# Linear attention and spectral mixing on one core: spectral weights loaded two modes at a time in 16 KB runs, with the two modes on row halves of TensorE

## The chip, the cores and the metric

The kernel runs on one core of a Trainium2 chip. The metric is the device time of one execution in microseconds (us). Each run also has a profiled span, which is about 1.8 us shorter than its time; the traces below are read in that span, and times "at" some microsecond count from its start. The granted clock is the share of full speed that the throttle gives TensorE.

Before the change the kernel took 427.29 us (median of 3 runs, 427.12 to 427.82).

## The reference

A linear attention (feature map elu + 1) makes x of 8 batches x 576 rows x 512 channels. A real Fourier transform along the rows follows; its first 64 modes are multiplied by complex 512 x 512 weights, one matrix pair per mode; the inverse transform is added to x, and a channel product with a rectifier ends it.

```python
x = attention(q, k, v)                     # 8 x 576 x 512
X = np.fft.rfft(x, axis=1)
Xr, Xi = X[:, :64].real, X[:, :64].imag
Yr = einsum('bmd,mde->bme', Xr, w_r) - einsum('bmd,mde->bme', Xi, w_i)
Yi = einsum('bmd,mde->bme', Xr, w_i) + einsum('bmd,mde->bme', Xi, w_r)
Y[:, :64] = Yr + 1j * Yi                   # the other modes are zero
u = x + np.fft.irfft(Y, n=576, axis=1)
return u + np.maximum(u @ w_ch, 0.0)
```

The weights are 64 modes x 2 matrices x 1 MB of float32, 134 MB of the 164 MB that the core reads.

## The kernel before

Three stages overlap. The *first stage* (to about 103 us) makes x batch by batch and transforms it. The *weights stage* multiplies mode after mode, as the weights arrive. The *tail* handles the last modes and the output after the last weights have landed.

A weight load is 1 MB, cast from float32 to bf16 on its way, on the gpsimd queue. Each partition receives four matrix rows, an 8 KB run in memory. Twelve buffers are filled in the first stage, eight more ("keep") stay in use to the end.

```python
    W_KEEP = 8
    def w_load(kk, half, pool, tag, bufs):
        name, src = (("wr", moe_w_r), ("wi", moe_w_i))[half]
        w = pool.tile([128, NDC, D], BF16, tag=tag, bufs=bufs, name=f"{name}{kk}")
        rows_of = src[kk].rearrange("(p dc) e -> p dc e", dc=NDC)          # NDC = 4
        for dcs in (slice(0, 3), slice(3, 4)) if (kk, half) == (NM - 1, 1) else (slice(0, NDC),):
            tc.keep_in_program_order(nc.gpsimd.dma_start(out=w[:, dcs], in_=rows_of[:, dcs, :]))
        return w
    W_PRE = 12
```

The transform of a batch puts channel 4p + dc on partition p of channel group dc. A group is five matmuls: four over 128 rows of x, and one over the 64 rows that are left of 576. The stationary operand (the one that TensorE loads before it streams the other) is x itself, every fourth channel.

```python
    def transform(b, dc):
        # ... cut: xf = a PSUM tile [128, 4, 2, 64]; half = the 64 partitions that hold the left rows
        o = xf[:, dc].rearrange("p t m -> p (t m)")
        for jj in range(NJJ):                                              # NJJ = 4
            pin(nc.tensor.matmul(o, x16[:, jj, dc::NDC], fwd_sb[:, jj, :], start=(jj == 0), stop=False))
        pin(nc.tensor.matmul(o, x16t[half, dc::NDC], fwd_sb[half, NJJ, :], start=False, stop=True))
        if dc == NDC - 1:
            # ... cut: two copies to xt_c, as bf16 (real, imaginary, minus imaginary)
```

The products of a mode are 8 matmuls of 128 rows x 32 columns, four of which stand side by side in the array. A product's four blocks are then added up by a 16-column "row-pick" matrix.

```python
    def mode_product(kk, ps, stage, yt_ps):
        wr, wi = w_get(kk)
        P = ps.tile([128, D], F32, tag="P", bufs=2, name=f"P{kk}")
        for t, w in ((1, wr), (0, wi)):
            for dc in range(NDC):
                fixed(nc.tensor.matmul(P[dc * 32 : dc * 32 + 32, :], xt_cols(dc, t, kk), w[:, dc, :],
                                       start=(t == 1), stop=(t == 0), tile_position=(0, dc * 32)))
            # ... cut: other work and warming matmuls
        # ... cut: P copied to st, on VectorE for even modes and ScalarE for odd ones
        for ec in range(NDC):
            fixed(nc.tensor.matmul(yt_ps[:, ec, kk % 8, :], st[:, ec * 128 : ec * 128 + 128], pick_sb))
```

The row-pick matrix is loaded on the gpsimd queue after all the prefetched weights:

```python
    while pending:
        w_next()
    tc.keep_in_program_order(nc.gpsimd.dma_start(out=wch16, in_=moe_w_ch.rearrange("(c p) j -> p c j", p=128)))
    tc.keep_in_program_order(nc.gpsimd.dma_start(out=pick_sb, in_=pick_dr.ap()))
```

Of the kernel before, what the change touches and what calls it, by code (L numbers as in the profile page):

```python
# [20 lines left out]
def _dft_consts(S: int, NM: int):  # L21

    m = np.arange(NM)
    s_cols = np.concatenate([4 * np.arange(128) + jj for jj in range(4)] + [512 + np.arange(NP)])
    s_rows = np.concatenate([s_cols, s_cols[512:]]).reshape(5, 128).T
    ang = 2.0 * np.pi * s_rows[:, :, None] * m / S
    fwd = np.concatenate([np.cos(ang), -np.sin(ang)], axis=2)

    scale = np.where(m == 0, 1.0, 2.0) / S
    ang = 2.0 * np.pi * np.outer(m, np.arange(S)) / S  # L30
    inv = np.empty((NM, 2, S), dtype=np.float64)
    inv[:, 0, :] = np.cos(ang) * scale[:, None]
    inv[:, 1, :] = -np.sin(ang) * scale[:, None]
    pick = np.zeros((128, 16), dtype=np.float16)
    for quad in range(4):
        for c in range(16):
            pick[quad * 32 + c, c] = 1.0

    return fwd.astype(np.float16), inv.reshape(2 * NM, S).astype(np.float16), pick
# [3 lines left out]
def kernel(  # L43
# [18 lines left out]
    XDC = 3 * B * NM  # L62
    XTW = NDC * XDC + 2 * B * NM
# [15 lines left out]
    fwd_sb = const.tile([128, 5, 2 * NM], F16, name="fwd_sb")  # L79
# [7 lines left out]
    nc.vector.memset(xt_c[:, NDC * XDC : XTW], 0.0)  # L87
    xt_v = xt_c[:, 0 : NDC * XDC].rearrange("p (c t b m) -> p c t b m", c=NDC, t=3, b=B)

    def xt_cols(dc: int, t: int, kk: int):  # L90

        c0 = dc * XDC + t * B * NM + kk
        return xt_c[:, c0 : c0 + 31 * NM + 1 : NM]
# [7 lines left out]
    W_KEEP = 8  # L101

    def w_load(kk: int, half: int, pool, tag: str, bufs: int):
        name, src = (("wr", moe_w_r), ("wi", moe_w_i))[half]
        w = pool.tile([128, NDC, D], BF16, tag=tag, bufs=bufs, name=f"{name}{kk}")
        rows_of = src[kk].rearrange("(p dc) e -> p dc e", dc=NDC)
        for dcs in (slice(0, 3), slice(3, 4)) if (kk, half) == (NM - 1, 1) else (slice(0, NDC),):
            tc.keep_in_program_order(nc.gpsimd.dma_start(out=w[:, dcs], in_=rows_of[:, dcs, :]))  # L108
        return w
# [4 lines left out]
    W_PRE = 12  # L114
# [170 lines left out]
    def transform(b, dc):  # L285
        if dc == 0:
            xfs[b] = psA.tile([128, NDC, 2, NM], F32, tag="xf", bufs=2, name=f"xf{b}")
        xf = xfs[b]
        o = xf[:, dc].rearrange("p t m -> p (t m)")
        half = HALVES[b % 2]  # L290
        x16, x16t = x16s[b]
        for jj in range(NJJ):
            pin(
                nc.tensor.matmul(
                    o, x16[:, jj, dc::NDC], fwd_sb[:, jj, :], start=(jj == 0), stop=False
                )
            )
        pin(
            nc.tensor.matmul(
                o, x16t[half, dc::NDC], fwd_sb[half, NJJ, :], start=False, stop=True  # L300
            )
        )
        if dc == NDC - 1:
            pin(nc.vector.tensor_copy(out=xt_v[:, :, 1:3, b, :], in_=xf))
            pin(nc.scalar.mul(out=xt_v[:, :, 0, b, :], in_=xf[:, :, 1, :], mul=-1.0))
# [7 lines left out]
    for b in range(B):  # L313
        if b + 2 < B:
            load(b + 2)
            if b >= 1:
                w_next()
# [29 lines left out]
    FILL = {61: (2, 2, 1), 62: (5, 3, 3), 63: (6,)}  # L347

    def mode_product(kk: int, ps, stage, yt_ps):

        wr, wi = w_get(kk)
        st = stage.tile([128, D], F16, tag="ystage", bufs=2, name=f"ys{kk}")
        fixed = pin if kk >= NF else (lambda ins: ins)
        fill = FILL.get(kk, (0, 0, 0))
        P = ps.tile([128, D], F32, tag="P", bufs=2, name=f"P{kk}")
        for t, w in ((1, wr), (0, wi)):
            for dc in range(NDC):
                fixed(
                    nc.tensor.matmul(  # L359
                        P[dc * 32 : dc * 32 + 32, :], xt_cols(dc, t, kk), w[:, dc, :],  # L360
                        start=(t == 1), stop=(t == 0), tile_position=(0, dc * 32),
                    )
                )
            if t == 1:
                work_slot(kk, 0)
                keep_warm(fill[0])
        if kk % 2 == 0:
            fixed(nc.vector.tensor_copy(out=st, in_=P))  # L368
        else:
            fixed(nc.scalar.copy(out=st, in_=P))  # L370
        work_slot(kk, 1)
        keep_warm(fill[1])
        for ec in range(NDC):
            fixed(
                nc.tensor.matmul(  # L375
                    yt_ps[:, ec, kk % 8, :], st[:, ec * 128 : ec * 128 + 128], pick_sb
                )
            )
# [10 lines left out]
    def last_mode(ps):  # L389

        kk = NM - 1
        wr, wi = w_get(kk)
        y_last = ps.tile([128, NDC, 2 * B], F32, tag="P", bufs=2, name="y_last")

        def product(t, w, dcs):
            for dc in dcs:
                c0 = dc * XDC + t * B * NM + kk
                x = xt_c[:, c0 : c0 + (2 * B - 1) * NM + 1 : NM]
                for ec in range(NDC):
                    pin(  # L400
                        nc.tensor.matmul(
                            y_last[:, ec, :], w[:, dc, ec * 128 : ec * 128 + 128], x,
                            start=(t == 1 and dc == 0 and ec == 0), stop=(t == 0 and dc == NDC - 1),
                            skip_group_check=True,
                        )
                    )

        product(1, wr, range(NDC))
        keep_warm(FILL[kk][0])
        product(0, wi, range(3))  # L410
        product(0, wi, range(3, NDC))
        nc.vector.tensor_copy(out=Y8[:, :, NL - 1, :], in_=y_last)
# [14 lines left out]
    n_early = n_keep + n_pre  # L427
# [28 lines left out]
    def mode(kk: int):  # L456
        nonlocal yt_ps
        if kk % 8 == 0:
            yt_ps = psW.tile([128, NDC, 8, 2 * B], F32, tag="yt", bufs=1, name=f"yt{kk // 8}")
        if kk == NM - 1:  # L460
            last_mode(psW)
            return
        mode_product(kk, psW, ystage, yt_ps)
        if kk == NM - 2:
            pin(nc.vector.tensor_copy(out=Y8[:, :, 0 : NL - 1, :], in_=yt_ps[:, :, 0 : NL - 1, :]))
        elif kk % 8 == 7:
            if kk < NF:
                nc.vector.tensor_copy(out=YE_T[:, :, kk - 7 : kk + 1, :], in_=yt_ps)
            else:
                g = (kk - NF) // NL + 1  # L470
                pin(nc.vector.tensor_copy(out=YL[:, :, :, g, :], in_=mode_rows(yt_ps)))

    for kk in range(n_early):
        mode(kk)
# [232 lines left out]
    QUADS = (5, 6)  # L707
# [52 lines left out]
    for kk in range(n_early, NM):  # L760
        mode(kk)
        if kk < NF:
            for i in spread(len(tiles), kk - n_early, NF - n_early):
                attention_rows(tiles[i])
        if kk == NE + 4:
            assert not work
            psB.release()
            acc_pools.append(
                tc.alloc_tile_pool(name="psT0", bufs=1, space=PSUM, side="right", reuse_waits="tile")
            )  # L770
            per_slot[NE + 5] = [1, 1]
            for n in range(N_PRE):
                work.append(lambda n=n: channels(n))

# [100 lines left out]
```

## Time and profile before

| | before |
|---|---|
| profiled span | 425.4 us |
| queue of the loads, share of 16 engines | 98.3% |
| written by the DMA engines, 160 to 340 us | 213 GB/s |
| transform of one batch (20 matmuls), clock 0.5 | 3.1 us |
| first product of the weights stage | 103.4 us |
| last product of the last mode | 393.1 us |
| from there to the end | 32.3 us |

The page of the kernel before. Part 2 cuts the span into 40 slices and gives the busy share in tenths per engine and the bytes written; part 3 lists the DMA queues with packets, MB and share of 16 engines; part 4 is the chain of waits that ended last, by engine.

```profile
PE   1358777887119765666333689778677778998992
...
DVE  4598999956002755556200433433444244421793
...
GB/s 215 208 208 209 209 210 209 212 212 215 218 211 214 214 212 215 214 213 214 212 214 213 213 214 213 214 214 213 213 213 214 214 213 213 213 213 157 250 394 295
...
q0 software_dynamic: 31360, 81.48, 98.3%
...
DMA 69%; PE 12%; issue 8%; DVE 7%; ACT 2%; POOL 1%; DVEq 0%; POOLq 0%; ACTq 0%
```

The gpsimd queue is busy for 98% of the span, at a level rate from the start to about 390 us (the last packet of the weights ends at 392.7 us), and 69% of the chain of waits is DMA. So the loads bound the kernel, and TensorE and VectorE may be late as long as the queue does not run empty. In the first stage VectorE is the busier one, as the windows of the kernel before show (columns: window, its length, busy us and instructions of PE, weight loads, VectorE, ScalarE and GpSimd, then granted clock, DMA share and GB/s written):

```profile
60.00:100.00 40.00, 30.56 (x434) 23.58 (x429) 32.62 (x64) 21.60 (x29) 9.73 (x17) 0.66 1.13 211
...
160.00:340.00 180.00, 118.71 (x935) 59.42 (x934) 71.56 (x173) 46.37 (x81) 38.12 (x72) 0.72 1.06 213
```

```profile
395.00:400.00 5.00, 4.75 (x22) 2.05 (x20) 3.96 (x6) 3.92 (x8) 0.56 (x1) 1.00 0.68 206
```

### The profile page before, as it was taken

To read this page: it belongs to the slowest core of one execution; us is meant where nothing else is said; L and a number is where in the kernel's file an instruction comes from. 1 tells how busy PE (TensorE), PEld (TensorE's weight loads), DVE (VectorE), ACT (ScalarE), POOL (GpSimd) and SP (SyncE) were. 2 spreads that over 40 slices of the span, in tenths; PEclk is the share of its full clock that TensorE was granted. 3 is DMA by queue.
4 is the path that set the end of the run, shared out by engine and by line. 5 is a ranking of instruction groups with operands and counts; after the bars stand their busy time and mean duration, and the time that the engine had idled before them with its cause. 6 is when DMAs were issued, how large, how long until landed. Compare 5 with 4: busy or idle time off the path is not lost.

```text
span 425.4 us, 6619 instructions
## 1 busy us (share of the span) xinstructions
PE 285.7 (67%) x2692; PEld 160.0 (38%) x2692; DVE 214.5 (50%) x440; ACT 154.1 (36%) x241; POOL 88.3 (21%) x159
## 2 busy tenths in 40 slices
PE   1358777887119765666333689778677778998992
PEld 0246555674003433333111334434334334473420
DVE  4598999956002755556200433433444244421793
ACT  4677776630102100000000244434443354430781
POOL 4222223222201322122112122112122121110000
PEclk9999866565555855555555587989999899999998
DMA  9999999999999999999999999999999999998797
GB/s 215 208 208 209 209 210 209 212 212 215 218 211 214 214 212 215 214 213 214 212 214 213 213 214 213 214 214 213 213 213 214 214 213 213 213 213 157 250 394 295
DMA packets 35502, 93.12 MB, mean 219 GB/s; under 512 B 3024, under 2 KB 15696, under 8 KB 35216
## 3 DMA queue, kind: packets, MB, share of 16 engines
q0 software_dynamic: 31360, 81.48, 98.3%
q1 hardware_dynamic: 4112, 11.22, 7.1%
q8 instruction: 21, 0.34, 0.3%
q14 instruction: 9, 0.07, 0.0%
HBM read 163.93 MB, written 9.44 MB: 407 GB/s over the span
## 4 chain that ended last, share of the span: by engine, by line
DMA 69%; PE 12%; issue 8%; DVE 7%; ACT 2%; POOL 1%; DVEq 0%; POOLq 0%; ACTq 0%
DMA wi<-in_moe_w_i_dram 51%; DMA wr<-in_moe_w_r_dram 9%; DMA k<-in_k_dram 9%; PE acc L641 3%; PE P L359 2%; DVE x L277 2%; PE acc L680 2%; ACT ke L190 1%; PE z L604 1%; DVE ke L203 1%; DVE k L197 1%; PE zb L631 1%; PE zb L630 1%; DVE qe L203 1%; PE yb L626 1%
## 5 line engine op out<-in xcount | busy, mean ns | idle before, releaser
L359 PE MATMUL P<-wi,xt_c 128*32 128x512 bf16 x252 | 37.9, 536 | 38.7 <-DMA wi<-in_moe_w_i_dram 38.6
L370 ACT CAST ys<-P 128x512 f16<-128x512 f32 x31 | 18.2, 586 | 121.6 <-PE P L359 106.8
L108 POOL DMA_DIRECT2D wr<-in_moe_w_r_dram x64 | 34.1, 533 | 130.6 <-PE P L359 91.0
L368 DVE CAST ys<-P 128x512 f16<-128x512 f32 x32 | 22.1, 691 | 72.0 <-PE P L359 49.8
L108 POOL DMA_DIRECT2D wi<-in_moe_w_i_dram x65 | 34.6, 532 | 111.8 <-PE P L359 88.2
L359 PEld LDWEIGHTS <-xt_c 128*32 128x32 bf16 x504 | 28.7, 156 | 75.8 <-issue 64.4
L359 PE MATMUL P<-wr,xt_c 128*32 128x512 bf16 x252 | 37.6, 550 | 24.6 <-DMA wr<-in_moe_w_r_dram 22.5
L563 DVE TENSOR_TENSOR x_main<-ya,x_main 128x512 f32<-128x512 f32 x32 | 22.1, 691 | 43.7 <-PE ya L559 43.6
L582 PE MATMUL eps<-wch,xTw 128*128 128x512 f16 x144 | 41.2, 414 | 0.0
L144 PEld LDWEIGHTS <-qT 64*128 64x128 f16 (+1 forms) x640 | 25.3, 126 | 41.6 <-issue 21.3
L565 ACT CAST x16w<-x_main 128x512 f16<-128x512 f32 x32 | 19.8, 618 | 37.4 <-DVE x_main L563 37.4
L375 PE MATMUL yt<-pick_sb,ys 128*128 128x16 f16 x252 | 16.6, 176 | 24.1 <-DMA pick_sb<-row_pick 15.2
L590 ACT CAST E<-eps 128x512 f16<-128x512 f32 (+1 forms) x40 | 21.3, 543 | 25.5 <-PE eps L582 25.5
L144 PE MATMUL num<-kv,qT 64*128 64x65 f16 (+1 forms) x320 | 13.8, 227 | 20.7 <-ACT kv L250 18.0
L375 PEld LDWEIGHTS <-ys 128*128 128x128 f16 x252 | 12.3, 103 | 39.8 <-issue 16.6
L190 ACT ACTIVATE qe<-q 128x1152 f16<-128x1152 f16 (+1 forms) x16 | 17.8, 1157 | 17.8 <-DMA q<-in_q_dram 17.8
L219 PE MATMUL qTp<-id,qe 128*128 128x128 f16 x144 | 16.7, 309 | 10.1 <-DVE qe L203 9.5
L144 PE MATMUL nw<-kv,qT 64*128 64x65 f16 (+1 forms) x320 | 22.1, 236 | 1.6 <-DVE x_tail L533 1.0
L277 DVE TENSOR_TENSOR x<-num,rd 128x512 f16<-128x512 f32 x32 | 22.1, 692 | 1.1
L190 ACT ACTIVATE ke<-k 128x1152 f16<-128x1152 f16 x16 | 17.7, 1155 | 6.6 <-DMA k<-in_k_dram 6.0
L690 ACT ACTIVATE acc<-acc 128x512 f32<-128x512 f32 x34 | 18.1, 581 | 2.3 <-PE acc L641 1.3
L219 PEld LDWEIGHTS <-qe 128*128 128x128 f16 x144 | 14.5, 146 | 11.2 <-DVE qe L203 9.9
(104 smaller groups left out, 442.5 us busy)
## 6 DMA issues: line engine op xcount, KB each, us to landing
wr<-in_moe_w_r_dram POOLq DMA_DIRECT2D x64, 512.0 KB, 18.6
wi<-in_moe_w_i_dram POOLq DMA_DIRECT2D x63, 512.0 KB, 18.7
k<-in_k_dram POOLq DMA_DIRECT2D x8, 576.0 KB, 14.5
v<-in_v_dram POOLq DMA_DIRECT2D x8, 576.0 KB, 16.6
out_dram<-x_main SPq DMA_DIRECT2D x9, 512.0 KB, 3.1
q<-in_q_dram POOLq DMA_DIRECT2D x7, 576.0 KB, 13.8
out_dram<-x_main SPq DMA_DIRECT2D x2, 1024.0 KB, 5.2
out_dram<-x_main SPq DMA_DIRECT2D x6, 256.0 KB, 3.4
```

Source lines behind the costliest of these rows:

```text
L108: tc.keep_in_program_order(nc.gpsimd.dma_start(out=w[:, dcs], in_=rows_of[:, dcs, :]))
L144: mm = nc.tensor.matmul(num[hpo][orow, c0 : c0 + 65], qT[rows, hpp, h2, cols], kv_sb[rows, hpp, h2, :])
L190: pin(nc.scalar.activation(out=ev[:, c], in_=heads(nm, b, c), func=AF.Exp))
L219: nc.tensor.transpose(qT_ps[:, j].rearrange("p t r -> p (t r)"), phi["q", b][:, hpp, j].rearrange("p o d -> p (o d)"), id16,)
L277: nc.vector.tensor_tensor(out=dst.rearrange("p (o c d) -> p o c d", o=2, c=4), in0=nv[:, :, :, 0:64], in1=rden.unsqueeze(3).broadcast_to([ ...
L359: nc.tensor.matmul(P[dc * 32 : dc * 32 + 32, :], xt_cols(dc, t, kk), w[:, dc, :], start=(t == 1), stop=(t == 0), tile_position=(0, dc * 32),)
L368: fixed(nc.vector.tensor_copy(out=st, in_=P))
L375: nc.tensor.matmul(yt_ps[:, ec, kk % 8, :], st[:, ec * 128 : ec * 128 + 128], pick_sb)
L563: pin(nc.vector.tensor_tensor(out=x, in0=acc, in1=x, op=ALU.add))
L565: pin(nc.scalar.copy(out=x16w[t], in_=x))
L582: nc.tensor.matmul(e_ps, xT[:, c, :], wch16[:, c, :], start=(c == 0), stop=(c == NDC - 1))
L590: pin(nc.scalar.copy(out=dst, in_=e_ps[:, cols]))
```

## The change

The intent: fewer and longer packets. Two modes are loaded at once, so that a partition receives eight matrix rows of one mode, a 16 KB run; even modes lie on partitions 0 to 63, odd ones on 64 to 127. 128 loads of 1 MB become 64 of 2 MB. The price is on TensorE. The channels of a mode now lie on 64 partitions (channel 8p + dc, eight groups), so the transform needs 80 matmuls of 64 columns per batch instead of 20 of 128, each with every eighth channel as stationary operand; and a pair of modes needs 32 product matmuls of 64 rows instead of 16 of 128. The last load comes in four pieces instead of two.

```diff
-    fwd = np.concatenate([np.cos(ang), -np.sin(ang)], axis=2)
+    fwd = np.stack([np.cos(ang), -np.sin(ang)], axis=2)
+    fwd = np.stack([fwd[..., 0::2], fwd[..., 1::2]], axis=2)
 ... cut
-    W_KEEP = 8
+    W_KEEP = 4
+    PIECES = (slice(0, 4), slice(4, 6), slice(6, 7), slice(7, 8))
-    def w_load(kk: int, half: int, pool, tag: str, bufs: int):
+    def w_load(kp: int, half: int, pool, tag: str, bufs: int):
-        w = pool.tile([128, NDC, D], BF16, tag=tag, bufs=bufs, name=f"{name}{kk}")
-        rows_of = src[kk].rearrange("(p dc) e -> p dc e", dc=NDC)
+        w = pool.tile([128, NDW, D], BF16, tag=tag, bufs=bufs, name=f"{name}{kp}")
+        rows_of = src[2 * kp : 2 * kp + 2].rearrange("k (p dc) e -> (k p) dc e", dc=NDW)
 ... cut
-    W_PRE = 12
+    W_PRE = 6
 ... cut: transform
-        for jj in range(NJJ):
-            pin(nc.tensor.matmul(o, x16[:, jj, dc::NDC], fwd_sb[:, jj, :], start=(jj == 0), stop=False))
-        pin(nc.tensor.matmul(o, x16t[half, dc::NDC], fwd_sb[half, NJJ, :], start=False, stop=True))
+        for dc in (2 * step, 2 * step + 1):
+            o = [xf[HALVES[h], dc].rearrange("p t m -> p (t m)") for h in range(2)]
+            for jj in range(NJJ + 1):
+                rows = half if jj == NJJ else slice(0, 128)
+                x = x16t[half, dc::NDW] if jj == NJJ else x16[:, jj, dc::NDW]
+                for h in range(2):
+                    pin(nc.tensor.matmul(o[h], x, fwd_sb[rows, jj, h].rearrange("p t m -> p (t m)"),
+                                         start=(jj == 0), stop=(jj == NJJ), skip_group_check=True))
 ... cut: the products of a pair
-            for dc in range(NDC):
-                nc.tensor.matmul(P[dc * 32 : dc * 32 + 32, :], xt_cols(dc, t, kk), w[:, dc, :], ...)
+            for dc in range(NDW):
+                c = dc % NDC * 32
+                for h in range(2):
+                    nc.tensor.matmul(P[h][c : c + 32, :], xt_cols(dc, t, kp)[HALVES[h]], w[HALVES[h], dc, :],
+                                     ..., tile_position=(h * 64, c), skip_group_check=True)
 ... cut
-    FILL = {61: (2, 2, 1), 62: (5, 3, 3), 63: (6,)}
+    FILL = {NM // 2 - 2: (2, 2, 3), NM // 2 - 1: (4,)}
```

FILL counts the matmuls without use ("warming matmuls") that are meant to keep TensorE's clock up near the end; e10 and e11 below compare two counts. The cut parts carry the pairs through the rest of the kernel.

## The prediction

> **What bounds it now.** The loads on the gpsimd queue. The page gives that queue 98% of 16 engines' span, and the chain of waits is 69% DMA. From 20 to 390 us the trace's packet records never show fewer than 16 packets in flight: no engine idles. In the weights stage (windows 160 to 380 us) 213 GB/s are written, 426 GB/s read, since the load halves float32 to bf16. The last weights land at 393 us; the 32 us after it (output) are untouched.
>
> **Cost of one load.** In the packet records a 2,304-byte read takes 107 ns, an 8,192-byte read 324 ns, a completion packet 22 ns. That is 22 ns + 0.0369 ns/byte: 434 GB/s for 16 engines, which agrees with the 435 GB/s fabric ceiling in the Trainium skill ("DMA: Bandwidth & Descriptors", "Where 436 GB/s comes from"). A 1 MB load (8 packets and a completion per engine) takes about 2,461 ns, less than 8 x 324 + 22 = 2,614, so each packet hides about 19 of its 22 ns. Left over the pure byte time are 8 x 3 + 22 = 46 ns per load. The same sum gives 2,835 ns for the q, k, v loads; their 208 GB/s agree. So the queue is within 2% of its ceiling; the prize is small.
>
> **On the critical path.** 128 loads become 64 of twice the size: a saved completion and, if a 16 KB run stays one packet, eight saved packets per pair. Estimate 64 x 46 ns = 2.9 us. If runs are cut back to 8 KB (the same page, "SDMA does more than copy", names 2,048 elements as the limit of one unit, CCE; no trace here shows whether it holds for a casting load), only completions are saved: 1.4 us.
>
> **Off the critical path.**
> - Products: 32 matmuls of 64 rows per pair in place of 16 of 128. Four old ones run together in 0.40 us at full clock (timeline). Eight tiles should run together: neutral.
> - Transforms: 80 half-size matmuls a batch in place of 20. Old: 3.1 us a batch at clock 0.65; estimate 4 to 6 us. TensorE is 73% busy there, VectorE 95%, so the first stage may end 3 to 10 us later than 103 us. It has room: prefetched weights keep the queue filled to about 123 us, and q, k, v loads wait 11 us behind others.
> - Buffers: 4 of 2 MB instead of 8 of 1 MB. When one is freed three stand queued, 14.7 us; TensorE lags 1 to 5 us in the busiest part. Enough.
> - Tail after the last landing: 8 small matmuls for 4, two parallel evictions: +0.2 us. Fewer warming matmuls may cost clock there: up to 2 us, unlikely.
>
> **Prediction.** 427.3 - 2.3 (between the two cases) + 0.2: 425.2 us, range 423.0 to 428.0. Faster by over 2%: 0.02; within 2%: 0.94; slower by over 2%: 0.04.
>
> **What would show it.** Right: written rate in the weights windows rises from 213 to about 215 GB/s; weight packets of 8,192 written bytes at about 626 ns; last weights land near 390.5 us; at least 16 packets in flight throughout; 32 us of tail. Split case: 4,096-byte packets remain, rate about 214.
>
> **What would make it wrong.** Gaps in the queue before 125 us because the transforms made TensorE the limit of the first stage (slower by several us); products of 64 rows running in turn, so that TensorE, 85 to 100% busy from 350 us, frees buffers late; a clock drop before the tail; long packets sharing engines unevenly.

## More of the kernel before

The timeline of TensorE in the kernel before, at the end of the first stage (start and length in us; the lengths of matmuls overlap, so read the distance between starts):

```profile
100.56 0.62 PE L294 MATMUL xf<-fwd_sb,x 128*128 128x128 f16 x4
...
101.34 0.62 PE L294 MATMUL xf<-fwd_sb,x 128*128 128x128 f16 x4
101.89 0.29 PE L299 MATMUL xf<-fwd_sb,x16t 64*128 64x128 f16 x1
103.38 0.68 PE L359 MATMUL P<-wr,xt_c 128*32 128x512 bf16 x4 [1.20 <-ACT xt_c L305]
```

One channel group, five matmuls, takes 0.78 us from start to start (100.56 to 101.34) at clock 0.5. The first product starts 1.5 us after the last transform.

The timeline of GpSimd's issues in the kernel before. In brackets stands how long it sat idle and what released it:

```profile
111.04 0.53 POOL L108 DMA_DIRECT2D wr<-in_moe_w_r_dram  x1 [2.21 <-DMA wr<-in_moe_w_r_dram]
...
127.84 0.54 POOL L108 DMA_DIRECT2D wr<-in_moe_w_r_dram  x1 [8.90 <-PE rows L512]
...
140.40 0.53 POOL L108 DMA_DIRECT2D wr<-in_moe_w_r_dram  x1 [9.71 <-PE P L359]
```

The load at 111.04 us is the 21st, so the first that needs a used buffer (20 are prefetched). The first two modes are multiplied at 103.4 to 105.3 us, which frees four buffers, and the loads into them go out from 111.04 to 118.41 us, held only by the queue itself. The two later lines are loads that do wait for a buffer. The queue stays filled meanwhile: no slice up to 380 us falls below 208 GB/s.

The tail of the kernel before, as the instructions on the result tile of the last mode (shortest, median and longest ns, first and last start), and the clock after it in the windows:

```profile
L401 PE MATMUL y_last<-xt_c,wi x16: 188/192/193, 392.4 to 393.1; 128*128 128x16 bf16 x16
```

## The result, and the profile after

| | before | after |
|---|---|---|
| time, median of 6 runs (lowest to highest) | 427.56 us (427.12 to 428.33) | 435.02 us (433.90 to 436.72) |
| profiled span | 425.4 us | 432.2 us |
| share of the load queue | 98.3% | 94.2% |
| written, 160 to 340 us | 213 GB/s | 216 GB/s |
| transform of one batch at clock 0.5 | 3.1 us | 7.05 us |
| first product of the weights stage | 103.4 us | 127.3 us |
| last product of the last mode | 393.1 us | 399.0 us |
| from there to the end | 32.3 us | 33.2 us |

The changed kernel is slower by 1.7%, so still within 2%: ratio 1.0173, 95% interval 1.0149 to 1.0198. A ratio here and below is the mean time of the one kernel's runs over the mean of the other's runs of the same rounds, so not quite the ratio of the medians. Executions over 1.5% slower than the fastest of the same kernel are left out of the means.

The page of the changed kernel, with the same lines as above except the chain of waits, which breaks off early in this profile (its shares sum to 10% of the span) and is not used:

```profile
PE   1259999999989855555523387887597768996992
...
DVE  4595787766321536546530153444245333531794
...
GB/s 215 207 208 212 207 214 205 217 215 215 215 106 196 207 207 215 214 218 215 215 216 215 216 217 213 216 216 217 214 217 215 217 215 215 215 215 134 221 400 304
...
q0 software_dynamic: 22432, 81.47, 94.2%
```

The queue's rate is up in the weights stage (mostly 214 to 217 where mostly 213 or 214 stood), with far fewer packets, and one slice has a hole: 106 GB/s, from 119 to 130 us. In the eight slices before it PE stands at 9, and VectorE, which had mostly stood at 9 in the first of them, is at 5 to 8. The windows of the changed kernel say the same in numbers:

```profile
60.00:100.00 40.00, 38.03 (x532) 33.31 (x530) 29.94 (x56) 21.63 (x27) 9.26 (x15) 0.56 1.11 213
100.00:120.00 20.00, 19.33 (x274) 16.74 (x274) 8.81 (x20) 3.43 (x6) 0.00 (x0) 0.59 1.03 216
120.00:130.00 10.00, 8.80 (x105) 6.03 (x106) 2.72 (x14) 0.73 (x3) 0.96 (x2) 0.50 0.51 93
130.00:150.00 20.00, 17.75 (x237) 6.57 (x235) 5.56 (x12) 5.17 (x12) 2.13 (x5) 0.50 1.01 206
160.00:340.00 180.00, 112.44 (x1276) 51.80 (x1275) 76.99 (x196) 43.14 (x77) 19.56 (x37) 0.68 1.03 216
```

TensorE is busy for 38.0 of 40 us between 60 and 100 us (30.6 before), and for nearly all of the next 20 us, in which the kernel before let it rest. The timeline of TensorE in the changed kernel, at the end of its first stage:

```profile
124.23 0.69 PE L302 MATMUL xf<-fwd_sb,x 128*64 128x64 f16 x8
...
125.11 0.69 PE L302 MATMUL xf<-fwd_sb,x 128*64 128x64 f16 x8
125.74 0.33 PE L302 MATMUL xf<-fwd_sb,x16t 64*64 64x64 f16 x2
127.27 1.09 PE L365 MATMUL P<-wr,xt_c 64*32 64x512 bf16 x16 [1.20 <-ACT xt_c L309]
```

A group of ten matmuls takes 0.88 us (124.23 to 125.11), so eight groups take 7.05 us per batch where four took 3.1. The first product comes at 127.27 us, 23.9 us later. The timeline of GpSimd's issues in the changed kernel shows what that does:

```profile
93.05 0.54 POOL L428 DMA_DIRECT2D pick_sb<-row_pick  x1 [4.20 <-DMA wi<-in_moe_w_i_dram]
128.69 0.53 POOL L112 DMA_DIRECT2D wr<-in_moe_w_r_dram  x1 [35.10 <-PE P L365]
...
133.76 0.53 POOL L112 DMA_DIRECT2D wr<-in_moe_w_r_dram  x1 [3.66 <-PE P L365]
...
148.68 0.53 POOL L112 DMA_DIRECT2D wr<-in_moe_w_r_dram  x1 [13.49 <-PE P L365]
```

From 93 us on every buffer has its load landed or queued. The first load into a used buffer goes out at 128.69 us, after the first products (in the kernel before, at 111.04 us); but the queue had run dry at about 123.5 us (171 GB/s in the window of 121 to 124 us, 10 GB/s in that of 124 to 127). A second, shorter hole lies near 147 us. There the early modes are worked off one pair every 3.56 us (product starts at 139.32, 142.88 and 146.44 us).

**Where the time went.** The bytes on the load queue, added up over the trace, give the lag of the queue without a model. The yardstick is kernel e10 below, the same loads with no hole. The changed kernel's queue is level with it at 20 MB, 6.8 us behind after the first hole (at 25 MB) and 7.9 us behind after the second (at 30 MB); it stays 7.8 us behind to the end. The kernel before is 2.8 us behind e10 at the end. So:

| term | us |
|---|---|
| longer packets, fewer completions | -2.8 |
| first hole | +6.8 |
| second hole | +1.0 |
| last pieces of the last load | +0.9 |
| tail after the last product | +0.9 |
| sum | +6.8 |

The difference of the profiled spans is 432.2 - 425.4 = 6.8 us. The lags are good to about 0.2 us. The fourth term is what is left between the queue (+5.0 us) and the last product (+5.9 us). Its cause is open. In the packet records a fetch of 16 KB of instructions on another queue, about 0.95 us long, falls on those last small pieces in the changed kernel (396.77 to 397.71 us; the last packet ends at 398.51); but such a fetch falls among the last small pieces of e10 too (388.43 to 389.37, last packet 389.78), of e1, s1 and s3, where these pieces are not late against the rest of the queue, and of the kernel before (last packet at 392.65 us; 392.63 in e2, which has no fetch there). So the fetch alone does not explain it.

The tail of the changed kernel, in the two views that were shown of before:

```profile
L408 PE MATMUL y_last<-xt_c,wi x64: 184/187/196, 396.3 to 399.0; 64*128 64x16 bf16 x64
```

```profile
395.00:400.00 5.00, 2.97 (x73) 1.86 (x72) 0.23 (x1) 0.24 (x2) 0.00 (x0) 0.59 0.30 52
```

The clock fell to 0.59 in those 5 us, where it had been 1.00: TensorE waits between four pieces with few warming matmuls. The four matmuls of the last channel product that follow take 1.06 us in the timeline, 0.60 us before.

### The profile page after: what moved, and what is told of

It reads as the page before. It is cut to its first block, busy times and chain, and to the rows that moved or that the text cites. A ratio compares the mean times of both kernels' runs of the same rounds, so it can differ in the third digit from the quotient of the medians.

```text
span 432.2 us, 8601 instructions
## 1 busy us (share of the span) xinstructions
PE 312.9 (72%) x3741; PEld 183.5 (42%) x3741; DVE 213.0 (49%) x439; ACT 153.5 (36%) x242; POOL 55.6 (13%) x97
## 2 busy tenths in 40 slices
DMA packets 26725, 93.24 MB, mean 216 GB/s; under 512 B 2048, under 2 KB 14848, under 8 KB 18496
## 3 DMA queue, kind: packets, MB, share of 16 engines
q0 software_dynamic: 22432, 81.47, 94.2%
## 5 line engine op out<-in xcount | busy, mean ns | idle before, releaser
L365 PE MATMUL P<-wr,xt_c 64*32 64x512 bf16 x496 | 34.6, 554 | 38.2 <-DMA wr<-in_moe_w_r_dram 34.6
L365 PE MATMUL P<-wi,xt_c 64*32 64x512 bf16 x496 | 32.0, 535 | 32.0 <-DMA wi<-in_moe_w_i_dram 32.0
L365 PEld LDWEIGHTS <-xt_c 64*32 64x32 bf16 x992 | 18.7, 147 | 80.1 <-issue 51.4
L591 PE MATMUL eps<-wch,xTw 128*128 128x512 f16 x144 | 44.4, 440 | 0.0
L302 PE MATMUL xf<-fwd_sb,x 128*64 128x64 f16 x512 | 44.2, 309 | 0.0
L112 POOL DMA_DIRECT2D wr<-in_moe_w_r_dram x32 | 17.4, 545 | 161.1 <-PE P L365 122.2
L302 PEld LDWEIGHTS <-x 128*64 128x64 f16 x512 | 35.9, 212 | 4.1
L112 POOL DMA_DIRECT2D wi<-in_moe_w_i_dram x35 | 18.6, 534 | 103.5 <-PE ya L568 38.9
L302 PE MATMUL xf<-fwd_sb,x16t 64*64 64x64 f16 x128 | 20.7, 321 | 0.0
L591 PEld LDWEIGHTS <-xTw 128*128 128x128 f16 x144 | 14.1, 110 | 15.2 <-issue 8.2
```

The costliest lines, as they stand in the source:

```text
L302: nc.tensor.matmul(o[h], x, fwd_sb[rows, jj, h].rearrange("p t m -> p (t m)"), start=(jj == 0), stop=(jj == NJJ), skip_group_check=True,)
L365: nc.tensor.matmul(P[h][c : c + 32, :], xt_cols(dc, t, kp)[HALVES[h]], w[HALVES[h], dc, :], start=(t == 1 and dc < NDC), stop=(t == 0 and ...
L591: nc.tensor.matmul(e_ps, xT[:, c, :], wch16[:, c, :], start=(c == 0), stop=(c == NDC - 1))
```

## The experiments

The expectations are quoted; they name theories by letter. A is that the longer transforms make the first stage late and the queue run dry. B, its rival, is that half as many buffers of twice the size come free too late or too coarsely. D, W and L in the last four runs are rival reasons for the price of one transform matmul. Times are medians of all runs of a kernel, with the lowest and highest in brackets; the kernel before ran in each set of rounds, at medians of 427.36 to 427.64 us.

### e1: the changed kernel with a shorter transform

Two of the five row blocks are multiplied, so 32 matmuls per batch instead of 80. The result is wrong; the comparison is too loose to see the spectral term.

```diff
-            for jj in range(NJJ + 1):
+            for jj in (0, NJJ):
```

> The changed kernel with each transform cut to 2 of its 5 row groups (32 matmuls a batch instead of 80, about 2.8 us instead of 7.05; the result is wrong on purpose, all loads, buffers and products unchanged). Theory A (the longer transforms make TensorE the limit of the first stage, so the first buffers are freed at 128.7 us, after the prefetched weights have run out at 123.5 us): the first stage ends near 103 us, no gap in the load queue, time 424.5 to 426.5 us. Rival B (4 buffers of 2 MB are freed too coarsely, or long packets share the engines badly): the gap near 125 to 150 us stays and the time stays at 432 us or more.

Measured: 427.69 us (427.45 to 428.48), ratio 1.0005 [0.9993, 1.0018]. The issues of e1 in the timeline of GpSimd:

```profile
109.34 0.53 POOL L112 DMA_DIRECT2D wr<-in_moe_w_r_dram  x1 [15.65 <-PE P L365]
...
128.90 0.53 POOL L112 DMA_DIRECT2D wr<-in_moe_w_r_dram  x1 [18.15 <-PE P L365]
...
143.81 0.53 POOL L112 DMA_DIRECT2D wr<-in_moe_w_r_dram  x1 [13.48 <-PE P L365]
```

The first hole is gone and about 7 us with it, with the loads, buffers and products of the change left alone: A holds for the first hole. The time expected was missed by 1.2 us, since the second hole grew. The queue ends 2.3 us behind e10, the tail's clock is low, and the gain of the packets is used up by that. The first buffers come free early here, but the next not before 128.90 us: the early products wait for the row-pick matrix, which lands at about 125 us, and then run at clock 0.50 (windows of 130 to 150 us).

### e2: the kernel before with a longer transform

Each channel group is multiplied two or three times over, 45 matmuls per batch instead of 20, with the right result.

```diff
-        for jj in range(NJJ):
-            pin(...)
-        pin(...)
+        for _ in range(3 if dc == 0 else 2):
+            for jj in range(NJJ):
+                pin(...)
+            pin(...)
```

> The kernel before with its transforms computed 2.25 times (45 matmuls a batch instead of 20, about 7.0 us; right result), loads and buffers as before. Theory A: the first stage ends near 125 us, a gap of 4 to 8 us in the load queue, time 432 to 437 us although no load was changed. Rival B: the queue stays full, time within 1 us of 427.5.

Measured: 426.95 us (426.86 to 427.02), ratio 0.9985 [0.9972, 0.9998]. A miss. The timeline of TensorE and a window of e2 say why:

```profile
107.21 0.41 PE L295 MATMUL xf<-fwd_sb,x 128*128 128x128 f16 x4
...
107.74 0.41 PE L295 MATMUL xf<-fwd_sb,x 128*128 128x128 f16 x4
...
109.53 0.47 PE L360 MATMUL P<-wr,xt_c 128*32 128x512 bf16 x4 [1.20 <-ACT xt_c L306]
```

```profile
60.00:100.00 40.00, 32.40 (x550) 25.31 (x551) 33.67 (x65) 22.68 (x30) 9.66 (x17) 1.00 1.13 211
```

The extra matmuls brought the clock from 0.66 to 1.00, and five of them then took 0.53 us instead of 0.78. The stage ended about 6 us later than before, not 24, and no hole came. So the count of matmuls alone is not the cost. What differs in the changed kernel is that its ten matmuls take 0.88 us at any clock: also between 33 and 43 us, where the clock is 1.00.

### e3 and e5: the kernel before with loads of two modes

These test B: 2 MB loads and half as many buffers, with the old transform and products. e3 keeps 8 KB runs and is right; e5 has the 16 KB runs of the change and is wrong (the rows of two modes get mixed).

```diff
+        w = pool.tile([128, 2, NDC, D], BF16, tag=tag, bufs=bufs, name=f"{name}{kp}")
+        rows_of = src[2 * kp : 2 * kp + 2].rearrange("k (p dc) e -> p k dc e", dc=NDC)            # e3
+        rows_of = src[2 * kp : 2 * kp + 2].rearrange("k (p dc) e -> (k p) dc e", dc=2 * NDC)      # e5
 ... cut: W_KEEP 4, W_PRE 6, one load per pair
```

> The kernel before with two modes per load (2 MB, 4 buffers instead of 8) but runs of 8 KB and the old layout, transforms and products. Theory A: no gap; only 64 completions of 22 ns are saved, time 1.0 to 1.8 us below before, written rate about 214 GB/s. Rival B (coarse buffers cause the gap): a gap appears and the time rises by 3 us or more.

> As the 8 KB pair load, but the loads are those of the changed kernel (16 KB runs, even modes on partitions 0 to 63), with the old transforms and products on it, so the result is wrong on purpose. Theory A: no gap, written rate about 216 GB/s, time 2.4 to 3.4 us below before (424.1 to 425.1). Rival C (long packets cost something themselves, for example uneven engines): no gain over the 8 KB runs, or a loss.

Measured: e3 433.55 us (428.52 to 436.05, two of six runs slow), ratio 1.0081 [1.0038, 1.0123] from the fast ones, which fall into two groups, near 428.5 and near 433.5 us (the profiled run is of the upper one); e5 429.92 us (427.35 to 432.39), ratio 1.0061 [1.0031, 1.0090]. Two windows of e5 and one of e3:

```profile
120.00:130.00 10.00, 4.93 (x42) 1.82 (x41) 0.69 (x1) 1.97 (x5) 0.89 (x2) 0.50 1.11 217
...
160.00:340.00 180.00, 116.15 (x928) 55.76 (x929) 71.11 (x170) 45.79 (x82) 19.03 (x36) 0.70 1.03 216
```

```profile
380.00:385.00 5.00, 5.00 (x52) 3.56 (x50) 0.85 (x2) 1.76 (x3) 1.45 (x3) 0.76 0.37 45
```

Neither has a hole at 123 us, so B does not explain the first one. Nor has either the second hole, though their row-pick matrix is as late (first used at 125.1 and 125.4 us); their clock from 130 to 140 us was 0.93 (e5) and 0.67 (e3), where the changed kernel had 0.50. The 16 KB runs bring the rate to 216 GB/s (e3: 214), which confirms the gain that the change was made for. But coarse buffers do cost something in *these* kernels: near the end, with the products still one mode at a time, a pair's buffer comes free late and the queue rests (45 GB/s in e3's window of 380 to 385 us). In the changed kernel both modes of a buffer are multiplied back to back, and no such hole is there.

### e6: e1 with the row-pick matrix loaded early

```diff
                 pin(nc.sync.dma_start(out=fwd_sb, in_=fwd_dr.ap()))
+                pin(nc.sync.dma_start(out=pick_sb, in_=pick_dr.ap()))
 ...
-    tc.keep_in_program_order(nc.gpsimd.dma_start(out=pick_sb, in_=pick_dr.ap()))
```

> The short-transform kernel of the first series (wrong on purpose) with one more edit: the 4 KB row-pick matrix is loaded at the start on the sync queue instead of behind all prefetched weights, so the early pairs need not wait for it until about 125 us. Theory A2 (what was left of the loss there was a second gap of 3.3 us near 144 us, because the early pairs are worked off too late, and a slow clock at the start of the tail): no gap before 390 us, time about 424.5 us (424.0 to 425.5). Rival B (coarse buffers themselves): the gap of about 3 us stays and so does 427.7.

Measured: 426.69 us (426.44 to 427.32), ratio 0.9983 [0.9971, 0.9995]. The second hole is gone: the windows from 120 to 150 us show 213 GB/s or more, and the queue is level with e10 to the end. The expected time was missed by about 1.2 us: the last piece comes 0.9 us later than in e10 (last packet at 390.71 us, last product at 391.5 us; why is open, see above), and the clock is 0.50 in the window of 390 to 395 us. With both holes removed the time falls below the kernel before, with a transform cut short; e10 below repeats it with a whole one.

### e4: the changed kernel with more warming matmuls near the end

```diff
-    FILL = {NM // 2 - 2: (2, 2, 3), NM // 2 - 1: (4,)}
+    FILL = {NM // 2 - 2: (2, 2, 8), NM // 2 - 1: (5,)}
-        for dcs in PIECES:
+        for i, dcs in enumerate(PIECES):
             product(0, wi, dcs)
+            keep_warm((2, 1, 0, 0)[i])
```

> The changed kernel with 9 more clock-keeping matmuls between the last two pairs and between the pieces of the last load. Theory A: the clock before the last landing stays at 1.00 instead of 0.59, the stretch from the last landing to the end is 32.4 us instead of 33.4, time 0.5 to 1.3 us below the changed kernel (433.7 to 434.5), with the gaps near 125 and 150 us unchanged. Rival: the time does not move, the tail is bound by VectorE.

Measured: 433.62 us (431.12 to 435.94), ratio 1.0141 [1.0115, 1.0166], which overlaps that of the change (1.0149 to 1.0198, in other rounds): inconclusive. The clock stayed at 1.00 until 400 us but fell to 0.66 in the next 5 us, after TensorE had waited 1.35 us for the last piece. The profiled run holds something else, which no edit made, as the edit lies near the end. Its clock happened to be high after the first hole:

```profile
130.00:150.00 20.00, 13.18 (x262) 6.68 (x261) 7.21 (x15) 5.33 (x12) 3.09 (x6) 0.93 1.02 204
```

Its queue, 7.2 us behind e10 after the first hole, was only 0.2 us further behind at 30 MB, where the changed kernel at clock 0.50 lost 1.0 us. This is one execution, but it suggests that the slow clock has a large part in the second hole.

### e7 and e8: full-width transforms, with x written in another order

Here x is written so that each group's 128 channels lie side by side; 20 full-width matmuls per batch do, and copies move halves of the result across partitions. e8 adds the early row-pick load and the warming.

```diff
+        dv = dst.rearrange("p (u o c e) -> p o c e u", u=NDW, o=2, c=4)
+        for o in range(2):
+            pin(nc.vector.tensor_tensor(out=dv[:, o], in0=..., in1=..., op=ALU.mult))
 ... cut
-                x = x16t[half, dc::NDW] if jj == NJJ else x16[:, jj, dc::NDW]
+            x = x16t[half] if jj == NJJ else x16[:, jj]
+            pin(nc.tensor.matmul(o, x[:, g * 128 : g * 128 + 128], fwd_sb[rows, jj]..., ...))
```

> The changed kernel with 20 full-width transforms a batch again (right result): the channels are permuted when x is written, and four half-partition copies, two of them from one row half to the other, put even modes on rows 0 to 63 and odd ones on 64 to 127. Theory A (number of weight loads of the half-width transforms is what made the first stage long; loads and buffers are innocent of the first gap): first stage ends before 110 us, no gap near 125 us, the second gap of 2 to 4 us stays, time 426.5 to 428.5 us. Rival (moving data between row halves costs as much): the stage stays beyond 120 us and the time above 432.

> Full-width transforms, early row-pick matrix and warm tail together, 16 KB loads kept (right result). Theory A: no gap in the load queue before the last landing, 216 GB/s written, last weights near 390.3 us, tail 32.5 us, time 424.3 to 425.3 us, 0.5 to 0.8% below the kernel before. Rival B: one of the gaps comes back and the time stays at or above 427.

Measured: 485.88 us (485.69 to 486.22), ratio 1.1366 [1.1351, 1.1381], and 486.74 us (483.69 to 488.35), ratio 1.1370. Both failed. The groups of instructions of e7 on VectorE:

```profile
L283 DVE TENSOR_TENSOR x<-num,rd 128x256 f16<-128x256 f32 x64 | 78.0, 1406 | 1.6
```

Two such writes, whose neighbours lie 128 bytes apart, take 2.8 us where one contiguous write of 128 x 512 took 0.69 us. VectorE, in the kernel before already 95% busy from 30 to 60 us, became the bound, and the queue stood empty for tens of microseconds. Moving a stride from one engine to another can be dearer than the stride.

### e10 and e11: the transform swapped

The transform first runs with the Fourier matrix as stationary operand (five matmuls of 512 columns), ScalarE copies the result, and 16 half-width matmuls with the identity turn it. e10 also loads the row-pick matrix early; e11 adds the warming.

```diff
+                pin(nc.tensor.matmul(xfs[b], fwd_sb[rows, jj].rearrange("p h t m -> p (h t m)"),
+                                     x16t[half] if jj == NJJ else x16[:, jj],
+                                     start=(jj == 0), stop=(jj == NJJ)))
 ... cut: after the five, on ScalarE
+                pin(nc.scalar.copy(out=xms[b], in_=xfs[b]))
 ... cut: for dc in the 8 groups, for h in both halves
+                pin(nc.tensor.matmul(xf[HALVES[h], dc].rearrange("p t m -> p (t m)"),
+                                     xms[b][:, dc::NDW], id16[:, h * 64 : h * 64 + 64], ...))
 ... cut: e11 only
-    FILL = {NM // 2 - 2: (2, 2, 3), NM // 2 - 1: (4,)}
+    FILL = {NM // 2 - 2: (2, 2, 8), NM // 2 - 1: (5,)}
+            keep_warm((3, 1, 1, 0)[i])
```

> The changed kernel with the same layout and loads (right result), but each batch's transform made in another order: 5 wide matmuls (Fourier matrix stationary, 512 channels moving) give modes on rows, one ScalarE copy rounds them to fp16, and 16 half-width matmuls with the identity put channels back on rows, even modes low and odd modes high; 21 weight loads a batch instead of 80, about 3.5 us instead of 7.05. The row-pick matrix is loaded at the start. Theory A: first stage ends before 110 us, no gap in the load queue near 125 or 145 us, 216 GB/s written, time 425.0 to 427.0 us, below the kernel before by up to 0.6% and 7 to 10 us below the changed kernel. Rival B (the coarse buffers are to blame): a gap of 3 us or more remains and the time is 428 or more.

> The swapped transform with more clock-keeping matmuls around the last pair. Theory A: clock 1.00 in the first 5 us after the last landing and a tail 0.5 to 1.0 us shorter than that of the swapped transform alone: 424.5 to 426.3 us. Rival: no difference beyond 0.3 us.

Measured: e10 425.54 us (425.26 to 426.31), ratio 0.9960 [0.9945, 0.9974]; e11 423.83 us (423.73 to 429.10), ratio 0.9938 [0.9901, 0.9975]. Five of e11's six runs lie within 0.14 us, the sixth at 429.10 us. The issues and windows of e10, then the tail of e11:

```profile
111.91 0.53 POOL L112 DMA_DIRECT2D wr<-in_moe_w_r_dram  x1 [23.03 <-PE P L380]
...
123.25 0.53 POOL L112 DMA_DIRECT2D wr<-in_moe_w_r_dram  x1 [9.93 <-PE P L380]
```

```profile
120.00:130.00 10.00, 9.25 (x104) 3.27 (x97) 1.38 (x2) 2.89 (x8) 1.06 (x2) 0.50 1.10 216
```

```profile
L423 PE MATMUL y_last<-xt_c,wi x64: 184/187/196, 387.6 to 390.2; 64*128 64x16 bf16 x64
```

```profile
395.00:400.00 5.00, 5.00 (x25) 1.60 (x23) 4.56 (x5) 4.25 (x9) 0.00 (x0) 1.00 1.00 361
```

With the buffers free in time there is no hole, and the last product starts at 390.2 us, 2.9 us before that of the kernel before. e11 keeps the clock at 1.00 there, and its tail takes 31.8 us instead of e10's 33.3 us. e11 is the fastest version found, with the right result.

### v1 and v2: does the swapped transform compute the same?

As the comparison is loose, the Fourier matrix was multiplied by 20 in the kernel before (v1) and in e10 (v2), on purpose wrong.

```diff
-    return fwd.astype(np.float16), ...
+    return (20.0 * fwd).astype(np.float16), ...
```

> A check of arithmetic, not of time: the kernel before with its forward Fourier matrix times 20, wrong on purpose. It gives a large relative error, which the swapped kernel with the same factor must repeat.

> The swapped transform with the same factor 20, wrong on purpose: if the new transform computes the same, its relative error agrees with that of the kernel before times 20 to about three digits. The comparison with the reference alone is too loose to show it: the short transform passed it with three fifths of its sum missing.

Measured: relative errors against the reference of 0.37870 and 0.37871, in one run each, at 427.25 and 425.06 us. The enlarged spectral term is the same in both to four digits, so e10's transform is right.

### s1 to s4: why ten transform matmuls take 0.88 us

That the transforms cause the first hole was shown, but not why one costs 88 ns whatever the clock. W: half width itself. L: the stationary operand's stride, now 16 bytes from channel to channel (8 before). D: each change between matmuls of 128 rows and of 64 rows, two per channel group and so sixteen per batch instead of eight. s1 puts the 64-row matmuls of a batch at its end (right result); s2 adds the early row-pick load and the warming; s3 takes 64 channels side by side (wrong order); s4 makes s1's change in the kernel before (right result).

```diff
 # s1 (and s2)
-        for dc in (2 * step, 2 * step + 1):
-            for jj in range(NJJ + 1):
+        parts = [(dc, jj) for dc in (2 * step, 2 * step + 1) for jj in range(NJJ)]
+        if step == NDC - 1:
+            parts += [(dc, NJJ) for dc in range(NDW)]
+        for dc, jj in parts:
-                            start=(jj == 0), stop=(jj == NJJ), skip_group_check=True,
+                        start=((dc, jj) == (0, 0)), stop=(jj == NJJ), skip_group_check=True,
 # s3
-                x = x16t[half, dc::NDW] if jj == NJJ else x16[:, jj, dc::NDW]
+                x = x16t[half, dc * 64 : dc * 64 + 64] if jj == NJJ else x16[:, jj, dc * 64 : dc * 64 + 64]
```

> The changed kernel with the same 80 half-width transform matmuls per batch, but the 16 matmuls of 64 rows (the tail rows of a batch) at the end of the batch and not after every channel group; right result. Theory D (going from 128-row to 64-row matmuls and back makes TensorE wait, about 0.14 us each way, and a half-width matmul itself takes only 60 ns; worked out from 10 matmuls in 0.88 us in the changed kernel and 4 in 0.52 us in e1): 80 x 60 ns and one pair of changes, 5.0 to 5.3 us per batch instead of 7.05; the first stage ends at 109 to 113 us instead of 126; the first buffer comes free at 111 to 115 us instead of 128.7; no gap of the queue at 123 to 130 us, the gap of 2 to 3.5 us near 145 us stays (row-pick matrix still late); 427.0 to 429.0 us. Theory W (88 ns is the price of a half-width matmul) and theory L (of its strided stationary operand): 88 ns each as before, stage end 126 us, 433.5 to 436 us.

> s1 with the row-pick matrix loaded at the start and the longer warming of e11; right result. Theory D: no gap before 385 us, last product at 390.0 to 391.5 us, clock 1.00 after it, 423.5 to 425.5 us, equal to e11 within 0.3%: the swapped transform of e11 is not needed, only the order. Theories W and L: the gap at 123 to 130 us stays, 429 to 432 us.

> The changed kernel with the 64 stationary columns of each transform matmul taken side by side instead of every eighth (16 bytes apart); channels in the wrong order on purpose. Theory L: 10 matmuls in 0.60 to 0.72 us instead of 0.88, stage end 110 to 118 us. Theories D and W: 0.86 to 0.90 us, stage end 124 to 126.5 us, 433 to 436 us.

> The kernel before with the 4 tail matmuls of 64 rows of a batch at the end of the batch; right result. Theory D, from 5 matmuls in 0.775 us at clock 0.5 and 0.525 us at clock 1.0: 107 ns per full-width matmul at clock 0.5 and 0.24 us for a pair of changes, so the last batch, whose groups stand together, takes 20 x 107 ns + 0.24 us, 2.3 to 2.5 us, instead of 3.1. Theories W and L: 3.1 us. All: the time stays, 426.5 to 428.3 us, as the transforms are not what bounds this kernel.

Measured: s1 429.43 us (428.74 to 429.62), ratio 1.0043 [1.0028, 1.0058]; s2 427.54 us (426.15 to 430.83), ratio 1.0007 [0.9977, 1.0036]; s3 429.29 us and s4 426.93 us in one run each, whose state is unknown. The timelines of TensorE at the end of the first stage, s1 and then s3:

```profile
108.59 1.17 PE L303 MATMUL xf<-fwd_sb,x16t 64*64 64x64 f16 x16
109.69 4.05 PE L303 MATMUL xf<-fwd_sb,x 128*64 128x64 f16 x64
113.67 1.17 PE L303 MATMUL xf<-fwd_sb,x16t 64*64 64x64 f16 x16
```

```profile
103.53 0.43 PE L302 MATMUL xf<-fwd_sb,x 128*64 128x64 f16 x8
103.89 0.26 PE L302 MATMUL xf<-fwd_sb,x16t 64*64 64x64 f16 x2
104.08 0.43 PE L302 MATMUL xf<-fwd_sb,x 128*64 128x64 f16 x8
...
106.99 1.09 PE L365 MATMUL P<-wr,xt_c 64*32 64x512 bf16 x16 [1.21 <-ACT xt_c L309]
```

In s1 64 matmuls of 128 rows take 3.98 us (109.69 to 113.67), 62 ns each with one change of row size among them, at clock 0.5, and near 37 us, at clock 1.00, 64 ns. (Two matmuls, one per half of the result, start together; between changes these pairs start 120 ns apart at either clock.) The batch takes 5.1 us, as D expected. In s3 the ten matmuls of a group take 0.55 us (103.53 to 104.08) at clock 0.5 and 0.39 us near 100 us at clock 1.00. So W falls: half width has no such price of its own. L holds for the larger part: with the stride a matmul takes 62 ns at any clock, and without it the stream is faster and follows the clock (pairs 53 ns apart in s3 at clock 0.5, 31 ns at 1.00). A stride of 8 bytes does not do this: the full-width matmuls of s4 start 107 ns apart at clock 0.5 and 56 ns at 1.00.

D holds too: two changes of row size per group made 0.88 us out of 10 x 62 ns = 0.62 us, about 0.13 us each. The two add up. In s3's trace at clock 0.5 the starts lie 171 and 186 ns apart across the two changes, 118 and 133 ns more than the 53 ns of a pair; in the changed kernel 242 and 252 ns, 122 and 132 ns more than the 120 ns of a pair. So a change costs the same with and without the stride, two of them about 0.25 us per group, and the stride costs the difference of the groups, 0.88 - 0.55 = 0.33 us. e10's 16 strided matmuls, with one change at their end, take 1.08 us, 67 ns each, which fits. s4's last 16 matmuls of 128 rows took 1.66 us at clock 0.5, 104 ns each, and the last batch of 20 took 1.9 us by the starts instead of 3.1 (2.3 to 2.5 expected; the clock had begun to rise): in the kernel before, too, the changes cost about 0.25 us per group (0.78 us less 5 x 104 ns), unnoticed.

Both s1 and s3 lose the first hole. In both the second one remains (the queue ends 3.6 and 3.3 us behind e10), and in s1 the last transform ends at 114.8 us, somewhat later than the 109 to 113 us expected. s2 missed its time. Its first product comes at 115.9 us, its second hole does not close (the queue ends 1.7 us behind e10), and its runs scatter over 4.7 us, which the traces at hand do not explain. So the better order alone does not reach e11.

## Why the prediction was wrong

**The step that failed** is the term "Transforms: 80 half-size matmuls a batch in place of 20 ... estimate 4 to 6 us", and what was built on it, "the first stage may end 3 to 10 us later than 103 us. It has room". The transforms took 7.05 us per batch, and the first product came 23.9 us later. The other side of that comparison was right: the queue was said to be filled to about 123 us, and it ran dry at about 123.5 us. Room of 20 us met a delay of 24 us, and a used buffer is not free until its products have run, so the first issue came at 128.69 us. The estimate is 1.3 to 1.9 times the old time for four times as many matmuls of half the width, and the old 3.1 us, which it puts at clock 0.65, were measured at 0.5. The runs showed a price per matmul that does not follow the clock: 62 ns for 64 stationary columns read at 16-byte steps (s1, s3), plus some 0.13 us at each change between 128 and 64 rows (s1, s3). The Trainium skill has both facts, and the prediction draws on neither. "SBUF — State Buffer", under "Door 1: The DMA port swizzle", says that SBUF has 16-byte lines and that full rate needs at least two accesses to the same line. The kernel before took every fourth float16, two per line; the change takes every eighth, one per line. "TensorEngine Tiling (Array Packing)", "Key Properties", says that "Changing tiling mode (not just tile) drains the TensorE". s3 and s1 agree with each page's direction; that the line and the drain are the mechanisms is the pages' word, the runs show the two costs.

**One thing was not foreseen at all**: the second hole (+1.0 us), as far as the traces show because the early modes are worked off late and slowly, at clock 0.50. It was not in the sum, nor in the list of what could go wrong. No edit took it away alone, but in e4's profiled run, at clock 0.93, it shrank to 0.2 us. Where the first hole was closed, it grew (e1, s1, s3), as the early modes then wait for the row-pick matrix; with that matrix early as well it was gone (e6, e10) or smaller than in s1 (s2, 1.7 us; its first stage still ends later than e10's).

**The tail**: "+0.2 us", with the clock term "up to 2 us, unlikely". It came: +0.9 us at clock 0.59, and e11 shows that more warming matmuls bring 1.5 us against e10. Another +0.9 us came from the last pieces; that was not foreseen, and its cause stays open (the instruction fetch that falls there falls there in runs without the delay too).

**What was right.** The gain on the queue: packets of 8,192 written bytes at 625 ns (626 predicted), 216 GB/s, and, once the holes were gone, the last product 2.9 us earlier (e10), which is the 64 x 46 ns of the unsplit case. The sum of 22 ns + 0.0369 ns per byte, 434 GB/s, still agrees with the 435 GB/s of the Trainium skill ("DMA: Bandwidth & Descriptors", "Where 436 GB/s comes from"); but the page works that figure out for the SBUF ports, while the 434 GB/s are bytes read and only half as many are written, so that this is the limit met here is not shown. The products: 32 half-height matmuls in place of 16 did not slow the weights stage (TensorE busy 112 us between 160 and 340 us, 119 before). The buffers: four of 2 MB sufficed in the layout of the change once the holes were gone (e10, e6), where both modes of a tile are used together; in e3 and e5, where they are not, they did not. And the first point under "What would make it wrong" named the event: holes before 125 us because the transforms make TensorE the limit of the first stage. It had been seen as a risk, and sized too small. e2's miss shows that this was no matter of counting: 2.25 times the full-width matmuls did no harm, as they raised the clock.

## What to carry to other kernels

A gain on a full queue lasts only as long as the queue never runs dry: compare the moment when the prefetched loads end with the moment when the first buffer comes free, and give the difference the error of the worst-known term in it. When a layout change alters the stride or the row count of a matmul's operands, do not scale the old duration by size; a stride that leaves one element per 16-byte line, or an order that alternates row sizes, can set a price that the clock hardly changes (the stride here cost the same at 0.5 and 1.00). Measure such a stream from start to start on a version that is allowed to be wrong, before building the rest on it.

## What the Trainium skill lacked or had wrong

- "SBUF — State Buffer", "Door 1: The DMA port swizzle": the sentence that one can stride for free by "4 fp32, 8 bf16, 16 int8" reads as if a step of 8 two-byte elements cost nothing. A matmul whose 64 stationary columns lie 8 float16 elements apart took 62 ns at clock 0.5 and 64 ns at 1.00 (s1), against 55 and 39 ns, changes of row size included, with the columns side by side (s3). "TensorE: Matmul & The Clock Gate", "LDWEIGHTS (loading the stationary operand)", gives the load time by columns alone, with no word on stride.
- "TensorEngine Tiling (Array Packing)", "Key Properties": no figure for the drain at a change of mode. Here a change between matmuls of 128 and of 64 rows cost about 0.13 us at clock 0.5, with strided operands (the changed kernel) and without (s3), and 0.25 us per pair of changes in the kernel before.
- "DMA: Bandwidth & Descriptors": it does not say how long a run of a casting load may be in one packet. 16 KB read and 8 KB written stayed one packet of 625 ns; the 2,048 elements that "SDMA does more than copy" names for CCE did not bind.
- "VectorE: DVE Perf Modes" names unit stride only as a condition of the faster modes and has no price for a strided destination (another page of the skill prices strided streams, but for 4-byte words). A product read from PSUM and written at a step of 128 bytes took 1,406 ns for 128 x 256 elements (e7), four times as long per element as the contiguous write (692 ns for 128 x 512), though by the page's table such a product runs at 1x either way.
